# First attention of a fused attention and feed-forward kernel: a pair's sums behind the next pair's scores, loads ahead of them, a norm behind the last sums, and a load moved into the product

## The chip, the cores and the metric

The kernel runs on one core of one Trainium2 chip. The metric is the device time of one execution in microseconds (us). Times are medians over several executions. One profiled execution gives a trace; its span (first to last instruction) is some 1.8 us shorter than its time. Engines: PE (TensorE), DVE (VectorE), ACT (ScalarE), POOL (GpSimd), and SP, the queue that issues most transfers.

## The reference, cut to what matters

```python
# q, k, v: (8, 12, 448, 64) float32; w_in (768, 2048), w_out (2048, 768)
q_n, k_n = rmsnorm(q, g_q), rmsnorm(k, g_k)
scores = q_n @ k_n.T / sqrt(64)
attn = softmax(scores)              # division by the sum over keys, + 1e-9
x = (attn @ v) brought to (8 * 448, 768)
out = relu(x @ w_in) ** 2 @ w_out
```

## The kernel before

The work is done in spans of two batches. The two matrix products of a span are done with combined blocks, seven in place of eight; the combined weight blocks (`w1s`, `w2s`) are made once. So the first attention, 12 pairs of heads with nothing on PE but themselves, shares DVE, ACT and POOL with the making of the weights (`weights`, one quarter step, or tick, at a time). After it the first product starts, and PE is then full nearly all of the time (never idle from 220 to 1100 us).

The step of one pair, with the parts that the change touches:

```python
def norm(i):                                   # pairs 3 to 11 (first and later spans: other code)
    # ... ACT: squares
    nc.vector.tensor_reduce(rstd, ...)                                    # L694
    nc.vector.tensor_scalar(rstd, rstd, 1.0 / D, 1e-6, ALU.mult, ALU.add) # L695
    nc.gpsimd.tensor_tensor(flat, flat, mhalf[:SP, 0:4 * NJ], ALU.pow)    # L697
    nc.gpsimd.tensor_tensor(..q normalised.., ALU.mult)                   # L699

def add_up(i, c):                              # DVE: partial sums of the exponentials, L764
def total_of(i):                               # PE: sums over keys, by a matmul with ones, L815
def finish(i):                                 # DVE: 1/sum, spread, times the values, L828 to L835

def attention_alone():
    for i in range(NAT):                       # NAT = 12
        more = i + 1 < NAT
        scores(i, 0)
        scores(i, 1)
        # ... i == 0 apart
        if more:
            transpose(i + 1, 1, 0)             # k of the next pair
        if i + 3 < NAT:
            load(i + 3)
        values(i - 1, (2, 3))
        total_of(i - 1)
        add_up(i, 1)
        if i + 2 < NAT:
            norm(i + 2)
        elif not more:
            norm(NAT)                          # span 1's first pair
            load(NAT + 2)                      # span 1's third pair
        yield                                  # at each yield: one or two ticks of the weights
        if more:
            transpose(i + 1, 0, 0)             # q of the next pair: needs L699
        finish(i - 1)
        load_v(i + 1)
        yield
        scores(i, 2)
        scores(i, 3)
        values(i, (0, 1))
        yield
        if more:
            add_up(i, 2)
        combine_x(i - 1)
        # ...
        yield
    values(i, (2, 3))
    total_of(i)
    finish(i)
    combine_x(i)

# the first product, in turn with what is left of the weights
for u, _ in enumerate(first_product(work, 0)):
    # ...
    weights(min(ALL, EARLY + (ALL - EARLY) * (u - 1) // (N1 - 6)))   # EARLY = 4 * 12
```

Line numbers that the traces show: L749 scores, L737 transposes (copied by ACT, L739 and L741), L754 exponentials on ACT, L805 values, L815 sums, L764 adding up. The weights: L588, L593 and L598 on DVE, L563 and L569 on POOL. L646 loads a weight block (`sw`), L583 stores a finished group of blocks (`w1s`), L665 loads q and k of a pair of a later span.

## Time and profile before

| | kernel before |
|---|---|
| time, median (range) | 1401.76 us (1400.38 to 1402.51) |
| span of the profiled execution | 1402.8 us (its time: 1404.63) |
| PE busy | 98% |
| first matmul of the first product | 134.48 us |
| from there to the end | 1268.3 us |

From the table by stretches of time, the part after the attention (columns: stretch, length, PE, weight loads, DVE, ACT, POOL, clock of PE, DMA share, GB/s):

```profile
160.00:180.00 20.00, 19.52 (x52) 9.52 (x51) 15.18 (x20) 9.83 (x15) 17.18 (x18) 1.00 1.02 375
180.00:200.00 20.00, 19.44 (x52) 9.61 (x51) 13.96 (x18) 13.69 (x22) 15.82 (x16) 1.00 1.04 401
```

### The profile page before, as it was taken

Reading aid. Unit: us, or ns where it says so; the run is one execution under the profiler, and the core shown is the slowest. Engines: PE = TensorE matmul, PEld = TensorE weight load, DVE = VectorE, ACT = ScalarE, POOL = GpSimd, SP = SyncE. Lnnn points to the kernel's source line nnn. Section 1 sums busy time; section 2 is a strip of 40 time slices with the busy share of each in tenths; the row PEclk is TensorE's granted clock in tenths of the full one; section 3 lists DMA queues with packets and bytes.
Section 4 is the critical chain, followed back from the end, with each engine's and each line's share of the span. In section 5 each row is a group of like instructions: output and inputs, shape, how many; then the busy total and the mean of one; then the engine's idle time right before and its main releaser. Section 6 shows DMA issues by size and latency. Waiting matters only on the chain.

```text
span 1402.8 us, 14398 instructions
## 1 busy us (share of the span) xinstructions
PE 1378.1 (98%) x4426; PEld 635.5 (45%) x4426; DVE 814.3 (58%) x1404; ACT 420.3 (30%) x621; POOL 590.7 (42%) x400
## 2 busy tenths in 40 slices
PE   8989999999999999999999999999999999999997
PEld 3333444444444454544444455444444445554553
DVE  6989677589876234476767523457777633332111
ACT  7875555433322011233232011232323201110000
POOL 6998888544452022544353122445445302221000
PEclk9999999999999999999999999999999999999999
DMA  8676998645655333345565332344565343323443
GB/s 239 190 196 168 352 374 316 183 104 119 137 113 120 98 88 87 104 103 122 117 136 122 95 96 85 103 105 105 120 128 107 94 102 86 90 86 103 107 110 70
DMA packets 430914, 188.78 MB, mean 135 GB/s; under 512 B 277484, under 2 KB 428780, under 8 KB 430828
## 3 DMA queue, kind: packets, MB, share of 16 engines
q1 hardware_dynamic: 421228, 179.05, 49.3%
q10 hardware_dynamic: 9472, 8.72, 2.3%
q8 instruction: 37, 0.61, 0.2%
q14 instruction: 49, 0.40, 0.1%
q0 software_dynamic: 128, 0.00, 0.0%
HBM read 154.54 MB, written 33.16 MB: 134 GB/s over the span
## 4 chain that ended last, share of the span: by engine, by line
PE 89%; POOL 3%; DVE 3%; issue 1%; DMA 1%; ACT 1%; POOLq 0%; ACTq 0%
PE ps L1044 37%; PE pc L997 10%; PE pd L997 10%; PE pa L997 10%; PE sc L749 9%; PE pav L805 9%; PE pb L997 5%; DMA sw<-w1s 1%; DVE gT L764 1%; POOL rstd L697 1%; POOL gC L569 1%; POOL qk L699 1%; POOL gC L563 1%; DVE gC L598 0%; PE tot L815 0%
## 5 line engine op out<-in xcount | busy, mean ns | idle before, releaser
L1044 PE MATMUL ps<-gT,sw 128*128 128x448 f32 x768 | 299.2, 542 | 0.8 <-POOL gT L974 0.8
L719 POOL TENSOR_TENSOR half<-half,mhalf 128x28 f32<-128x28 f32 x36 | 173.6, 4824 | 262.3 <-DVE half L718 228.8
L1044 PE MATMUL ps<-gC,sw 128*128 128x448 f32 x576 | 225.2, 542 | 0.0
L974 POOL TENSOR_TENSOR gT<-gT 128x448 f32<-128x448 f32 x96 | 93.5, 976 | 311.9 <-ACT gT L970 311.9
L1044 PEld LDWEIGHTS ps<-gT,sw 128*128 128x128 f32 x768 | 143.9, 190 | 151.0 <-issue 146.5
L756 ACT ACTIVATE pr<-sc 112x896 f32<-112x896 f32 x120 | 104.8, 914 | 293.9 <-PE sc L749 201.7
L749 PE MATMUL sc<-qkT 64*112 64x448 f32 x768 | 171.5, 565 | 1.9 <-ACT gT L754 1.1
L1044 PEld LDWEIGHTS ps<-gC,sw 128*128 128x128 f32 x576 | 108.0, 190 | 112.3 <-issue 111.1
L997 PE MATMUL pa<-xT,sw 128*128 128x448 f32 x384 | 154.9, 539 | 0.5 <-DMA sw<-w1s 0.5
L970 ACT ACTIVATE gT<-gT 128x448 f32<-128x448 f32 x96 | 55.3, 576 | 312.6 <-DVE gT L1012 312.6
L749 PEld LDWEIGHTS sc<-qkT 64*112 64x112 f32 x768 | 61.2, 173 | 99.6 <-issue 81.5
L997 PEld LDWEIGHTS pa<-xT,sw 128*128 128x128 f32 x384 | 72.8, 190 | 72.5 <-issue 71.9
L805 PE MATMUL pav<-pr,vt 112*64 112x448 f32 x480 | 100.2, 547 | 0.0
L721 POOL TENSOR_TENSOR qk<-qk,half 128x448 f32<-128x448 f32 x72 | 84.3, 1191 | 2.8
L997 PE MATMUL pb<-xC,sw 128*128 128x448 f32 x192 | 77.6, 540 | 2.0 <-issue 1.5
L1012 DVE TENSOR_TENSOR gT<-z,pd 128x448 f32<-128x448 f32 x32 | 19.9, 621 | 102.2 <-PE pd L997 102.2
L764 DVE TENSOR_TENSOR acc<-acc,pr 112x896 f32<-112x896 f32 x60 | 68.3, 1138 | 18.4 <-ACT pr L756 15.9
L997 PE MATMUL pd<-xC,sw 128*128 128x448 f32 x192 | 77.5, 540 | 1.4 <-DMA sw<-w1s 1.3
L997 PE MATMUL pd<-xT,sw 128*128 128x448 f32 x192 | 78.0, 542 | 0.0
L997 PE MATMUL pc<-xC,sw 128*128 128x448 f32 x192 | 77.4, 539 | 0.0
L997 PE MATMUL pc<-xT,sw 128*128 128x448 f32 x192 | 77.4, 539 | 0.0
L569 POOL TENSOR_TENSOR gC<-gC 128x384 f32<-128x384 f32 x64 | 72.1, 1146 | 2.5
(120 smaller groups left out, 1565.7 us busy)
## 6 DMA issues: line engine op xcount, KB each, us to landing
sw<-w1s SPq DMA_DIRECT2D x224, 192.0 KB, 2.4
sw<-w2s SPq DMA_DIRECT2D x168, 256.0 KB, 3.3
w1s<-gC SPq DMA_DIRECT2D x8, 1344.0 KB, 7.5
w2s<-gC SPq DMA_DIRECT2D x8, 1344.0 KB, 5.7
out_dram<-osb SPq DMA_DIRECT2D x184, 56.0 KB, 1.9
qk<-in_q_dram SPq DMA_DIRECT2D x144, 56.0 KB, 3.0
qk<-in_k_dram SPq DMA_DIRECT2D x144, 56.0 KB, 2.9
vt<-in_v_dram SPq DMA_DIRECT2D x72, 112.0 KB, 2.9
```

Source lines behind the costliest of these rows:

```text
L569: nc.gpsimd.tensor_tensor(*[blocks_of(n)[:, i] for i in (dst, x, y)], op)
L719: nc.gpsimd.tensor_tensor(half, half, mhalf, ALU.pow)
L721: nc.gpsimd.tensor_tensor(qkn[:, s], raw[:, s], half[:, s * NG:(s + 1) * NG].rearrange("p g -> p g ()").to_broadcast([P, NG, 32]), ALU.mult)
L749: nc.tensor.matmul(sc[:, h, 0:S], qkT[rows, at, 1, c * SP:(c + 1) * SP], qkT[rows, at, 0, :], start=True, stop=True)
L756: nc.scalar.activation(pr, sc[:, :, 0:S], AF.Exp)
L764: nc.vector.tensor_tensor(acc, probs[i, 0] if c == 1 else acc, probs[i, c], ALU.add)
L805: nc.tensor.matmul(pavs[i][h * D:(h + 1) * D, :], vs[i][:, h, c, :], probs[i, c][:, h, :], start=(c == 0), stop=(c == NJ - 1))
L970: nc.scalar.activation(g, src, AF.Relu)
L974: nc.gpsimd.tensor_tensor(g, g, g, ALU.mult)
L997: nc.tensor.matmul(ps, stream[n + i][:, c], rhs[:, c], start=first and c == 0, stop=c == HC - 1, skip_group_check=not first)
L1012: add(g, x, ps, ALU.add)
L1044: nc.tensor.matmul(ps, stream[n][:, c % 4], rhs_of[i][:, c], start=c == 0, stop=c == HF - 1)
```

## The change

The intent: the sums over keys wait for DVE's adding up, so they go behind the next two scores; the loads go ahead of the scores; the norm of span 1's first pair leaves DVE's busy end of the attention; and the load that stood beside it goes into the product.

```diff
         for i in range(NAT):
             more = i + 1 < NAT
+            if 0 < i < NAT - 3:
+                load(i + 3)
             scores(i, 0)
             scores(i, 1)
 ...
             if more:
                 transpose(i + 1, 1, 0)
-            if i + 3 < NAT:
-                load(i + 3)
             values(i - 1, (2, 3))
-            total_of(i - 1)
             add_up(i, 1)
             if i + 2 < NAT:
                 norm(i + 2)
-            elif not more:
-                norm(NAT)
-                load(NAT + 2)
             yield
             if more:
                 transpose(i + 1, 0, 0)
-            finish(i - 1)
             load_v(i + 1)
             yield
             scores(i, 2)
             scores(i, 3)
+            total_of(i - 1)
             values(i, (0, 1))
+            finish(i - 1)
             yield
 ...
         finish(i)
         combine_x(i)
+        norm(NAT)
 ...
+                if u == 12:
+                    load(NAT + 2)
                 weights(min(ALL, EARLY + (ALL - EARLY) * (u - 1) // (N1 - 6)))
```

## The prediction

> **What bounds the kernel now.** I first read the page: TensorE (PE) is busy nearly throughout, so only its idle time can be won.
>
> ```profile
> PE 1378.1 (98%) x4426; PEld 635.5 (45%) x4426; DVE 814.3 (58%) x1404; ACT 420.3 (30%) x621; POOL 590.7 (42%) x400
> ```
>
> The span is 1402.8 us, so PE idles 24.7 us. The table by stretches of time says where: PE is short of full by 3.70, 1.99, 0.60, 0.50, 2.64, 3.52, 1.46, 1.30 us in the eight stretches of 20 us up to 160, 15.7 us in all; from 200 to 1200 it is never idle. The change touches just that part: the first attention (12 pairs, 9 to 134.5 us) and the head of the first product. So at most about 12 us (0.9%) can be had, since the first 3.7 us are start-up that the change leaves alone.
>
> Next, the same table shows what is full there:
>
> ```profile
> 40.00:60.00 20.00, 19.40 (x102) 7.20 (x100) 19.66 (x23) 16.35 (x28) 19.69 (x13) 1.00 0.58 173
> 60.00:80.00 20.00, 19.50 (x104) 7.38 (x102) 19.73 (x25) 16.79 (x28) 19.69 (x13) 1.00 0.65 186
> 100.00:120.00 20.00, 16.48 (x82) 5.90 (x82) 19.13 (x27) 12.55 (x22) 19.68 (x12) 0.95 0.54 148
> ```
>
> After the stretch and its length come PE, weight loads, DVE (VectorE), ACT, POOL (GpSimd), then PE's clock and the DMA share. PE, DVE and POOL are all full at once up to 80; from 100 to 120 PE has slack and POOL has none. The waits of PE from 0 to 260 us say what it sees:
>
> ```profile
> PE tot L815 <- DVE gT L764: 4.4, 5, 1.5
> PE pt L737 <- POOL qk L699: 2.2, 2, 2.0
> PE pb L997 <- issue: 1.5, 1, 1.5
> PE pd L997 <- DMA sw<-w1s: 1.3, 1, 1.3
> ```
>
> The first line is what the change aims at: the row sums (tot) wait for VectorE's adding up. The timelines of POOL and of PE around 116 us show who really sets the pace:
>
> ```profile
> 105.07 2.84 POOL L563 TENSOR_TENSOR gC<-gC 128x384 int32<-128x384 int32 x2
> 107.99 2.76 POOL L569 TENSOR_TENSOR gC<-gC 128x384 f32<-128x384 f32 x2
> 110.71 3.06 POOL L697 TENSOR_TENSOR rstd<-rstd,mhalf 112x16 f32<-112x16 f32 x1
> 113.85 2.64 POOL L699 TENSOR_TENSOR qk<-qk,rstd 112x512 f32<-112x512 f32 x1
> ...
> 112.82 1.68 PE L815 MATMUL tot<-gT,ones 112*64 112x448 f32 x8
> 116.55 0.60 PE L737 MATMUL pt<-ident,qk 112*128 112x112 f32 x4 [2.05 <-POOL qk L699]
> ```
>
> POOL runs without a gap: from 25.7 us (its first combined norm) to 127 it is idle only 0.54 us at 35 and 1.12 us at 86.9. A pair costs it a power (2.9 to 3.8), a normalising product (1.0 to 2.8) and four to six weight operations (1.0 to 2.0 each), 9.4 to 13.6 us; a pair costs PE 9.26 us (tot 70.69 to tot 79.95, no wait between). So PE can't run ahead: pair n's last transpose needs POOL's product (L699), which ends at 60.35, 71.7, 81.7, 91.5, 105.1 and 116.5 us. **POOL bounds the attention's second half**; the waits for tot are partly time that PE would have lost to POOL anyway.
>
> **What the Trainium skill says.** "SBUF — State Buffer", section "Who interferes with whom": a DVE instruction with two SBUF inputs contends with a GpSimd instruction that reads SBUF, and the later one blocks fully. The trace agrees: adding up (L764) takes 1.03 to 1.09 us where POOL is out of the way and 1.9 us where it isn't. So full DVE and POOL stretch each other; the change leaves the amount of such work alone. "TensorE: Matmul & The Clock Gate", "What's actually happening": activity sets the clock, over free-running windows of about 3.4 us. Here the granted clock was 0.54 and 0.61 in 118:120 and 120:122, after the wait of 2.05 us: the next 16 matmuls took 5.0 us in place of 3.3. "Trainium Kernel Development and Optimization", "Key Constraints": DMAs of all queues run on the same 16 engines; here weight blocks queue behind the 1344 KB stores, below.
>
> **The change, part by part.** The instruction order of the two kernels (compiled side by side) has the same instructions on every engine; only places differ.
>
> *Loads first.* In the SP queue's order no load of the first attention moves: the line moves within one step, and nothing else is issued in that step before it. Its waits (POOL's product, the reduce) stay too. Worth 0.
>
> *Sums behind the next scores.* PE's order per pair was scores, transpose, values, tot, transpose, scores, values; it becomes scores, transpose, values, transpose, scores, tot, values. Tot gains 2.2 us of room (transpose 0.53, scores 1.69), more than its longest wait of 1.53, so the 4.4 us vanish as named. But the transpose, which needs POOL, comes 1.65 us earlier and no longer has tot to fill its wait. Counting from each L699 end above: pair 6's transpose starts at 60.35, the next is ready at 69.6 and waits to 71.7 (2.1 us); the one after at 81.7 hardly waits; at 102.35 PE is ready and waits to 105.1 (2.8); at 114.6 it waits to 116.5 (1.9). After 116.5 PE owes, before: transpose 0.55, scores 1.69, values 1.65, scores 1.69, values 1.65, tot 1.67, scores 1.69, values 3.3, tot 2.45, sum 16.3, plus 1.6 of slow clock, 134.5. After: the same plus one tot, so the product starts near 136.2. **+1.7 us**, if POOL keeps its pace.
>
> *VectorE's tail.* finish of pair 9 started at 115.5, a little after its tot. Now that tot comes after the scores behind 116.5: with the slow clock 116.55 + 0.55 + 2.3 + 2.7 = 122. VectorE then does finish 2.5 (to 124.6) and all it did from 118.1 to 138.4 less the norm (2.5) and one wait (0.57), 17.2 us: finish of pair 11 ends at about 141.5 (140.2 at full clock) in place of 138.36. pb needs it: its bank held that pair's values, read at 137.40 to 138.36, and the wait of 1.5 before pb (138.46) is that. **pb at about 141, +2.6 us** in place of the hoped-for saving.
>
> *Norm behind the last sums.* It takes 2.5 us of VectorE and ACT's 1.9 us wait off that tail, counted above. But POOL's power (5.45) and products (1.84) now start at about 145 instead of 130.7, and stand in POOL's order before the totals of the next weight block. So the store of that block (issued 152.44) goes out at about 159, and the SP queue takes it before a block of weights:
>
> ```profile
> 152.44 0.41 SPq L583 DMA_DIRECT2D w1s<-gC  x1
> 153.80 2.57 SPq L646 DMA_DIRECT2D sw<-w1s  x2
> ...
> 153.80 9.51 DMA sw<-w1s
> 163.31 0.14 issue
> 163.44 1.74 PE pa L997 x4
> ```
>
> (timeline of the SP queue, then the chain of waits: issued 153.80, landed 163.31.) With 1.5 MB ahead at the 400 GB/s of this stretch, 3.8 us and some 2.5 more to land, that block comes at about 166 after the change: +2 to +3 us on 163.44. As PE is by then only level or 0.2 behind, this wait replaces the earlier delay and doesn't add to it.
>
> *The load moved to use 12.* It frees the SP queue of 3.9 us at 137 to 141, so the wait of 1.30 at 149 goes; this too is swallowed by the wait at about 164. At its new place (about 168 to 172) the DMA share is 1.0 and the eight small DMAs push weight blocks back; PE has five blocks of 2.25 us in hand. 0 to +1.
>
> **Sum.** +2.6 at the block that lands late, +0.5 for the moved load, -0.5 for the 0.56 us wait at 189 that may fall away: about +2.5 from the trace. Later code is the same and PE full, so it carries over one to one: 1401.76 + 2.5 = about 1404.
>
> **Rivals.** (a) *The intended gain comes*: tot's 4.4, pb's 1.5 and the DMA waits' 1.8 vanish, nothing takes their place, and no clock dip (1.6): 1401.8 - 9 = 1393 at best. For it: each wait is there by name. Against it: POOL's gapless chain to 116.5. Half of it, if POOL gets quicker by altered overlaps with VectorE, gives 1397 to 1399. (b) *It nets out*: the late store is hidden by better DMA order, the tail delay is 1 us: 1401 to 1402. (c) *The delays add*: late tail, late block, a second clock dip of 1.6 after the new 2.8 us wait at 102, and blocks starved by the moved load: 1408.
>
> **Range and chances.** Since the whole part holds 12 us of removable idle and the delays found are 1 to 6 us, nothing gets to 2% (28 us). I choose 1404.0 with 1398.5 to 1408.5; the low end covers half of rival (a). Faster by over 2%: 0.01; within: 0.98; slower: 0.01.
>
> **What would show it.** Right: PE's waits for tot near 0, its waits for POOL's L699 up from 2.2 to 5 us or more; L699's ends unchanged within 1.5 us; the product's first matmul at 135 to 137; pb at 140 to 142; a wait for a weight block of 2 to 4 us at about 164. Wrong: L699 ending for the last pair well before 116 (POOL was not the pace-maker), pb before 138, or the store that went out at 152.44 still going before 155.

## More of the kernel before

L997 (L995 or so in other kernels) is the first product.

## The result, and the profile after

The changed kernel is correct and takes 1408.77 us in the median (1408.30 to 1408.91, 4 runs), the kernel before on the same chip 1401.46 us (4 runs). A ratio here is of one kernel's runs to the other's of the same rounds, so it isn't quite the ratio of the medians quoted: 1.0052, with a 95% interval of 1.0034 to 1.0069, or some 7.3 us slower. That is within 2%, as predicted, but 0.27 us above the range given, and 4.8 us above the time given.

The profiled execution spans 1406.9 us. PE's line of the page:

```profile
PE 1377.0 (98%) x4426; PEld 636.0 (45%) x4426; DVE 812.7 (58%) x1404; ACT 420.4 (30%) x621; POOL 591.6 (42%) x400
```

The work is the same; the idle time of PE went from 24.7 to 29.9 us (1406.9 less 1377.0). The table by stretches says where (columns as above):

```profile
40.00:60.00 20.00, 20.00 (x104) 7.51 (x102) 19.62 (x22) 17.14 (x30) 19.46 (x12) 1.00 0.62 184
60.00:80.00 20.00, 18.18 (x96) 7.19 (x96) 19.66 (x22) 15.53 (x26) 19.66 (x12) 1.00 0.55 167
100.00:120.00 20.00, 17.30 (x92) 6.91 (x92) 16.58 (x22) 13.82 (x24) 19.69 (x12) 1.00 0.62 170
160.00:180.00 20.00, 16.29 (x42) 7.82 (x42) 13.73 (x19) 9.85 (x15) 19.53 (x20) 1.00 1.06 324
```

Two places are new: 60 to 80, where PE fell from 19.50 to 18.18 with DVE and POOL still full, and 160 to 180, where it fell from 19.52 to 16.29. What PE waits for (line, what released it, us in total, times, longest):

```profile
PE pt L737 <- POOL qk L699: 7.7, 6, 2.7
PE pd L995 <- DMA sw<-w1s: 3.1, 2, 2.4
PE pt L737 <- ACT qkT L739: 1.9, 1, 1.9
PE pa L995 <- ACT gT L968: 1.4, 1, 1.4
```

The waits for the sums (4.4 us before) are gone, and the waits for POOL's product took their place: 7.7 us where there were 2.2. The 1.9 us stand at 21 us, where the sums of the first pair used to fill a wait for ACT's copy. POOL still runs without a gap up to the last pair's product (timeline of POOL, then of PE):

```profile
105.36 2.84 POOL L563 TENSOR_TENSOR gC<-gC 128x384 int32<-128x384 int32 x2
108.29 2.76 POOL L569 TENSOR_TENSOR gC<-gC 128x384 f32<-128x384 f32 x2
111.01 2.91 POOL L697 TENSOR_TENSOR rstd<-rstd,mhalf 112x16 f32<-112x16 f32 x1
113.99 2.00 POOL L699 TENSOR_TENSOR qk<-qk,rstd 112x512 f32<-112x512 f32 x1
...
116.05 0.60 PE L737 MATMUL pt<-ident,qk 112*128 112x112 f32 x4 [1.26 <-POOL qk L699]
```

The second loss is in the SP queue (its timeline, then two links of the chain that ends in PE's wait at 198.00 us; that store went out as soon as POOL's work was done, and then took 10.46 us to land):

```profile
157.12 0.37 SPq L583 DMA_DIRECT2D w1s<-gC  x1
...
166.85 4.33 SPq L665 DMA_DIRECT2D qk<-in_q_dram  x4
171.23 3.35 SPq L665 DMA_DIRECT2D qk<-in_k_dram  x4
...
175.21 1.32 SPq L646 DMA_DIRECT2D sw<-w1s  x3
...
177.12 10.46 DMA w1s<-gC
187.64 10.22 DMA sw<-w1s
```

The moved load holds the queue for 7.7 us, at 166.85 to 174.6, in front of weight blocks. It took 3.9 us at its old place. The product runs short at 180.17 (2.44 us), 188.09 (0.92) and 198.00 (0.62).

### The profile page after: what moved, and what is told of

The parts are those of the page before. It is cut to its first block, busy times and chain, and to the rows that moved or that the text cites. A ratio compares the mean times of both kernels' runs of the same rounds, so it can differ in the third digit from the quotient of the medians. Undisturbed runs are those within 1.5% of the kernel's fastest.

```text
span 1406.9 us, 14401 instructions
## 1 busy us (share of the span) xinstructions
PE 1377.0 (98%) x4426; PEld 636.0 (45%) x4426; DVE 812.7 (58%) x1404; ACT 420.4 (30%) x621; POOL 591.6 (42%) x400
## 4 chain that ended last, share of the span: by engine, by line
PE 89%; DVE 4%; DMA 3%; ACT 1%; POOL 1%; issue 1%; SPq 0%; ACTq 0%; DVEq 0%; POOLq 0%
PE ps L1042 37%; PE sc L749 10%; PE pd L995 10%; PE pa L995 9%; PE pc L995 9%; PE pav L805 9%; PE pb L995 5%; DVE gT L764 1%; DMA qk<-in_k_dram 1%; DMA w1s<-gC 1%; DMA sw<-w1s 1%; PE tot L815 1%; DVE gC L598 1%; DVE rstd L694 0%; POOL rstd L335 0%
## 5 line engine op out<-in xcount | busy, mean ns | idle before, releaser
L764 DVE TENSOR_TENSOR acc<-acc,pr 112x896 f32<-112x896 f32 x60 | 68.2, 1136 | 18.1 <-ACT pr L756 15.6
L569 POOL TENSOR_TENSOR gC<-gC 128x384 f32<-128x384 f32 x64 | 76.6, 1216 | 2.5
```

Of the source, the lines that this page charges most:

```text
L569: nc.gpsimd.tensor_tensor(*[blocks_of(n)[:, i] for i in (dst, x, y)], op)
L764: nc.vector.tensor_tensor(acc, probs[i, 0] if c == 1 else acc, probs[i, c], ALU.add)
```

## The experiments

Every experiment below was timed in five rounds (c8 and s_early_fin have a sixth run; the changed kernel has four) against the kernel before on the same chip. Differences in us are the ratio less one, times 1402; the 95% intervals are about 1.9 us to each side (2.5 for the changed kernel). The ratios of the experiments agree with the listed times to 0.0001 when the first run of each list, the profiled one, is left out. With it, differences move by 0.8 us at most (e1_sums to +4.2, s_tail to +2.6). The kernel before itself spread from 1399.5 to 1405.1 us over all these runs.

| kernel | median us | ratio (95%) | difference | product starts | from there to the end |
|---|---|---|---|---|---|
| before | 1401.5 to 1402.8 | | | 134.5 | 1268.3 |
| changed | 1408.77 | 1.0052 (1.0034 to 1.0069) | +7.3 | 135.1 | 1271.9 |
| e1_sums | 1405.46 | 1.0025 (1.0011 to 1.0038) | +3.5 | 138.1 | 1268.2 |
| e3_load12 | 1404.67 | 1.0018 (1.0004 to 1.0031) | +2.5 | 133.5 | 1270.5 |
| e2_norm_load12 | 1404.59 | 1.0018 (1.0004 to 1.0031) | +2.5 | 131.3 | 1271.5 |
| f_load44 | 1401.72 | 0.9998 (0.9984 to 1.0012) | -0.3 | 131.4 | 1267.9 |
| f_all44 | 1405.01 | 1.0025 (1.0011 to 1.0039) | +3.5 | 135.1 | 1268.0 |
| s_head | 1405.25 | 1.0023 (1.0009 to 1.0036) | +3.2 | 136.1 | 1267.3 |
| s_tail | 1405.08 | 1.0024 (1.0010 to 1.0038) | +3.4 | (131.8) | (1266.9) |
| s_from2 | 1404.85 | 1.0023 (1.0010 to 1.0037) | +3.2 | 135.3 | 1268.7 |
| s_fin | 1406.53 | 1.0029 (1.0015 to 1.0043) | +4.1 | 138.4 | 1266.3 |
| s_early_fin | 1407.65 | 1.0034 (1.0019 to 1.0049) | +4.8 | 139.7 | 1266.8 |
| g_fast | 1402.12 | 1.0002 (0.9988 to 1.0016) | +0.3 | 131.3 | 1269.5 |
| g_sums_fast | 1398.15 | 0.9973 (0.9960 to 0.9987) | -3.8 | 127.8 | 1267.4 |
| c8 | 1398.13 | 0.9976 (0.9963 to 0.9989) | -3.4 | 122.1 | 1274.3 |
| c8_sums | 1400.93 | 0.9996 (0.9983 to 1.0010) | -0.6 | 124.4 | 1273.9 |
| c10_sums | 1401.98 | 0.9999 (0.9985 to 1.0013) | -0.1 | 132.6 | 1268.6 |
| c8_load44 | 1394.55 | 0.9944 (0.9930 to 0.9958) | -7.9 | 122.9 | 1269.8 |
| c10_load44 | 1393.30 | 0.9937 (0.9923 to 0.9950) | -8.8 | 126.6 | 1264.9 |
| c10_sumsy44 | 1397.13 | 0.9957 (0.9944 to 0.9970) | -6.0 | 132.3 | 1265.5 |

The last two columns are of the one profiled execution of each. That of s_tail was the odd one of its kernel (1400.49 us, the other four 1404.71 to 1406.43), so its columns stand in brackets and nothing is drawn from them.

A theory and two rivals stood at first: L, the load at use 12 costs most; S, the deferred sums cost most; N, the late norm does.

### One part at a time

"Loads ahead of the scores" alone needed no run: built alone, it gives the same instructions with the same waits on every engine as the kernel before.

**e1_sums**: sums and finish deferred, nothing else.

```diff
             values(i - 1, (2, 3))
-            total_of(i - 1)
 ...
-            finish(i - 1)
             load_v(i + 1)
             yield
             scores(i, 2)
             scores(i, 3)
+            total_of(i - 1)
             values(i, (0, 1))
+            finish(i - 1)
```

> Only the sums and the finish are put behind the next scores. Theory L (the load moved to use 12 costs most of the 7 us): +1 to +2 us on the kernel before, since the last pair's transpose still comes at about 116 us and one set of sums is now owed after it. Rival S (the deferred sums are the cost): +5 us or more. Rival N (the late norm is the cost): within 1 us of before. Waits of TensorE for tot near 0 in all three, waits for POOL's L699 above 5 us.

**e3_load12**: only the load moved to use 12.

```diff
                 norm(NAT)
-                load(NAT + 2)
 ...
+                if u == 12:
+                    load(NAT + 2)
```

> Only the third load of span 1 is moved to use 12 of the first product; norm and sums stay. Theory L: +2 to +4 us, with TensorE waiting 3 us or more for weight blocks between 170 and 200 us. Rivals S and N: -1 to 0 us, since the queue is freed at 137 us and the wait of 1.3 us at 149 goes.

**e2_norm_load12**: the same, and the norm behind the last sums (`+ norm(NAT)` after the last `combine_x`).

> The whole change without the deferred sums: norm behind the last sums, load at use 12. Theory L: +3 to +5 us. Rival S: within 1.5 us of before. Rival N: +5 us or more, and the difference to the run with the load alone at use 12 is 3 us or more.

**f_load44**: as e3_load12, with `u == 44` in place of 12.

> As the run before, but the load is moved to use 44 (about 235 us), where the DMA share falls below 1. Theory L: -1 to -2 us on before, 4 us or more better than with use 12. Rivals S and N: as with use 12, within 1 us.

Measured: +3.5, +2.5, +2.5 and -0.3 us. Rival N fell: with and without the late norm the time is the same. Theory L got its 2 to 4 us for the load, with waits for weight blocks of 2.4 us in place of 3 or more; rival S got less than its 5. So the loss has two parts of about the same size, deferral and load. They add to 6.0 of the 7.3, within the intervals. The last two columns of the table part them: with the load at use 12 the time from the product's start to the end is 1270.5 to 1271.9, without it, in all kernels with correct results and as much of the weights made early, 1266.3 to 1268.7. The deferral lies all in the product's start. e3_load12's PE timeline shows the short blocks at the places where the changed kernel has them:

```profile
176.40 2.49 PE L996 MATMUL pd<-xT,sw 128*128 128x448 f32 x6 [1.45 <-DMA sw<-w1s]
183.97 2.52 PE L996 MATMUL pc<-xT,sw 128*128 128x448 f32 x6 [0.57 <-DMA sw<-w1s]
193.88 2.49 PE L996 MATMUL pd<-xT,sw 128*128 128x448 f32 x6 [0.42 <-DMA sw<-w1s]
```

f_load44 missed what was expected of it, a gain of 1 to 2 us. It removes the cost of use 12 and no more, so the load at its old place cost nothing that can be measured.

**f_all44**: the whole change with the load at use 44.

> The whole change, but with the load of the first pair but two of span 1 at use 44 of the first product in place of use 12. If the parts add: 7.3 us (the whole change) less 2.9 us (use 12 against use 44, as measured on the kernel before) leaves +3.5 to +5 us against before. If the load at use 12 and the late norm only cost something because PE was already late, or the waits overlap: +6 us or more.

Measured +3.5, as the sum of the parts said; its PE has no wait for a weight block from 135 to 290 us. The load's place is thus worth 3.8 us within the change (0.0052 less 0.0025, times 1402). And the deferral with the late norm and the loads ahead costs what it costs alone (e1_sums, +3.5).

### Does POOL decide what the deferral is worth?

Theory P: the transposes need POOL's product, POOL is the pace, and a sum moved behind them only leaves the wait bare. Rival V: DVE and PE set the pace. Rival H: the early wait for ACT's copy at 21 us makes the cost.

**g_fast**: POOL's power on 4 of 16 columns, 1.25 us in place of about 3. Its output is wrong, which doesn't matter for the time.

```diff
-        nc.gpsimd.tensor_tensor(flat, flat, mhalf[:SP, 0:4 * NJ], ALU.pow)
+        nc.gpsimd.tensor_tensor(flat[:, 0:NJ], flat[:, 0:NJ], mhalf[:SP, 0:NJ], ALU.pow)
```

> The kernel before, with POOL's power on 4 of 16 columns of the norm of pairs 3 to 11 (wrong results on purpose), which takes some 2 us a pair from POOL and changes no other order. Theory P (POOL's gapless chain bounds the second half of the first attention): faster than before by 2 to 6 us, POOL idle before its powers, PE's waits for L699 near 0. Rival V (POOL is not the bound; VectorE and PE are): within 1 us of before.

**g_sums_fast**: the same, and the sums deferred as in e1_sums. Its output is wrong, which doesn't matter for the time.

> The same shortened power, with the sums deferred (wrong results on purpose); to be compared with g_fast. Theory P (deferred sums cost 3.4 us because the transposes then stand bare before POOL's product): with POOL relieved the deferral costs nothing or gains, g_sums_fast minus g_fast between -4 and +0.5 us. Rival V (the deferral costs by itself: one sum owed after the last transpose and VectorE's tail later): +2 to +4 us again. Rival H (the early wait of 1.94 us for ACT's copy and the slow clock after it): about +2.

Measured: +0.3 and -3.8. So half of theory P fell: relieving POOL alone brings nothing. The other half stood: with POOL relieved, deferring the sums is worth 4.1 us, where it costs 3.5 us without. The waits of PE in g_fast (first line) and in g_sums_fast (the other two) tell why:

```profile
PE tot L815 <- DVE gT L764: 6.5, 8, 2.0
...
PE pt L737 <- ACT qkT L739: 2.5, 1, 2.5
PE tot L815 <- DVE gT L764: 1.4, 2, 0.9
```

In g_fast no wait for POOL is left and the waits for the sums have grown from 4.4 to 6.5 us; DVE is busy 78.8 of the 80 us from 38 to 118 (74.2 in the kernel before). Part of that is stretching: the adding up takes 1.89 us in the mean, 1.60 in the kernel before. The product starts at 131.25 us, where f_load44, as fast as the kernel before, starts it at 131.43. DVE stands right behind POOL, the two are level as pace-makers, and taking one away shows the other. The deferral takes away the waits for DVE, and can win only where POOL doesn't give them back.

### Where in the deferral is the cost?

**s_head** and **s_tail**: the deferral for steps 1 to 6, or 7 to 11, alone (the old places if `i >= 7`, or `i < 7`).

> Sums and finish deferred for pairs up to 6 only (steps 1 to 6), correct results. Theory P (cost lies where PE waits for POOL, steps 7 to 11): 0 to +1 us against before. Rival H (cost comes from the early wait at 21 us): +2.5 to +3.5 us.

> Sums and finish deferred for steps 7 to 11 only, correct results. Theory P: +2.5 to +3.5 us against before. Rival H: 0 to +1 us.

**s_from2**: the deferral in all steps but the first.

> Sums and finish deferred in steps 2 to 11, step 1 as before. If the bare wait of step 1 makes the cost: at most +1.5 us against before. If POOL's chain or the late finish makes it: +2.5 to +3.5 us, as with all steps.

Measured +3.2, +3.4 and +3.2: neither theory for the halves, and for s_from2 the second of its alternatives. Rival H fell with s_from2, whose wait for ACT's copy is 0.8 us and whose cost is the same. The parts don't add up: each half costs as much as the whole. So it isn't a sum of bare waits, which my prediction had made it.

**s_fin**: PE's order as before, only finish moved.

```diff
             if more:
                 transpose(i + 1, 0, 0)
-            finish(i - 1)
             load_v(i + 1)
             yield
             scores(i, 2)
             scores(i, 3)
             values(i, (0, 1))
+            finish(i - 1)
```

> Only finish moved behind the values; the sums stay in their old place. If the late finish on VectorE (and what it overlaps on POOL) makes the cost: +2 to +3.5 us. If PE's order makes it (transposes bare, one sum owed): within 1 us of before.

**s_early_fin**: PE's order as in e1_sums, DVE's, POOL's and SP's orders as before (compared instruction by instruction). ACT's order is not as before: in seven steps four exponentials go ahead of an operation of the weights, so this run changes PE's order and a little of ACT's.

```diff
-            total_of(i - 1)
 ...
             if more:
                 transpose(i + 1, 0, 0)
+            scores(i, 2)
+            scores(i, 3)
+            total_of(i - 1)
             finish(i - 1)
             load_v(i + 1)
             yield
-            scores(i, 2)
-            scores(i, 3)
             values(i, (0, 1))
```

> Sums deferred behind the next pair's scores on PE, with VectorE's order as before: the two scores, the sums and finish stand ahead of the weights' step. If the late finish on VectorE made the cost: within 1.5 us of before, or faster by up to 2. If PE's order made it (bare transposes, a sum owed at the end): +2.5 to +3.5 us, as e1_sums.

Measured: +4.1 and +4.8. Finish moved alone costs all that the deferral costs, without any change to PE's order. And PE's order (with ACT's) costs it too with DVE's order untouched, where the theory of the late finish expected nothing. Neither is thus the cause by itself. The two have one thing in common: finish comes later on a DVE that has no time to give. In s_fin it slipped behind a step of the weights (L593, in some steps also L598) in DVE's order. In s_early_fin it kept its place in the order, so DVE stood still for it, 9.9 us in all (waits of DVE):

```profile
DVE gT L828 <- PE tot L815: 9.9, 6, 5.2
```

In the kernel before this wait doesn't show, and in f_load44 it is 0.2 us; in e1_sums, where finish both slips and waits, it is 7.3 us, in the changed kernel 4.1. What the slip does shows in the timelines of DVE and POOL at the same pair, 66 to 82 us; first f_load44, with finish (L828 to L835) at its old place:

```profile
66.99 1.08 DVE L764 TENSOR_TENSOR gT<-gT 112x896 f32<-112x896 f32 x1
68.45 1.09 DVE L764 TENSOR_TENSOR gT<-gT 112x896 f32<-112x896 f32 x1
70.41 2.35 POOL L569 TENSOR_TENSOR gC<-gC 128x384 f32<-128x384 f32 x2
71.82 0.64 DVE L828 STREAM_TRANSPOSE gT<-tot 128x448 f32<-128x448 f32 x1
```

and then s_fin:

```profile
67.94 0.64 DVE L828 STREAM_TRANSPOSE gT<-tot 128x448 f32<-128x448 f32 x1
70.41 1.47 DVE L764 TENSOR_TENSOR gT<-gT 112x896 f32<-112x896 f32 x1
70.88 4.14 POOL L569 TENSOR_TENSOR gC<-gC 128x384 f32<-128x384 f32 x2
72.27 1.90 DVE L764 TENSOR_TENSOR gT<-gT 112x896 f32<-112x896 f32 x1
```

With finish early, the adding up (L764, two inputs in SBUF) ran beside POOL's power and into its product and took 1.08 and 1.09 us (the product then took 1.77 us, in s_fin 1.04), and POOL's weights ran mostly beside DVE's transposes and reduces: 2.35 us for two. With finish late, it is finish that runs beside the power, and the adding up falls on POOL's weights: 1.47 and 1.90 us, and 4.14 for the two. This is what the Trainium skill's page "SBUF — State Buffer", section "Who interferes with whom", says of a VectorE instruction with two SBUF inputs beside a GpSimd instruction that reads SBUF: the two contend. The lines of the weights and of the product agree; beside the power, which reads SBUF too, no stretching shows (1.08 us, as with POOL idle at 23.2 us in the kernel before, 1.09). Over the stretch from 38 to 118 us (busy time of each group over its count, worked out from the timelines):

| mean us of one | finish at its old place (before, e2, e3, f_load44) | finish behind the values (changed, e1, s_fin, s_from2, f_all44) |
|---|---|---|
| DVE L764, adding up | 1.42 to 1.60 | 1.61 to 1.66 |
| DVE L598, weights | 0.95 to 0.99 | 1.23 to 1.28 |
| POOL L569, weights | 1.26 to 1.38 | 1.57 to 1.64 |
| POOL L699, product | 1.78 to 1.95 | 1.58 to 1.72 |
| POOL, end of the 2nd L699 to end of the last | 73.6 to 76.2 | 76.9 to 78.7 |

POOL's chain has the same instructions in the same order, with at most 1.4 us of waits in it, and is 2.4 us longer in the second group (the mean of 77.3 less that of 74.9). The two groups don't overlap, but 76.2 and 76.9 are close.

How a late POOL reaches the product shows in the SP queue. The v of the last pair stands there behind the loads of span 1's first pair, these behind a store of weights, and the store waits for two of POOL's totals (L569), which follow the last L699. First f_load44 (POOL, two lines of the queue, PE), then the changed kernel:

```profile
113.40 1.96 POOL L569 TENSOR_TENSOR gC<-gC 128x384 f32<-128x384 f32 x2
115.39 0.38 SPq L583 DMA_DIRECT2D w1s<-gC  x1
122.08 0.42 SPq L678 DMA_DIRECT2D vt<-in_v_dram  x1
125.37 3.73 PE L805 MATMUL pav<-gT,vt 112*64 112x448 f32 x16 [1.40 <-DMA vt<-in_v_dram]
...
115.95 3.68 POOL L569 TENSOR_TENSOR gC<-gC 128x384 f32<-128x384 f32 x2
119.66 0.38 SPq L583 DMA_DIRECT2D w1s<-gC  x1
126.35 0.42 SPq L678 DMA_DIRECT2D vt<-in_v_dram  x1
129.56 3.23 PE L805 MATMUL pav<-gT,vt 112*64 112x448 f32 x16 [1.38 <-DMA vt<-in_v_dram]
```

From the store to this v it is 6.7 us in all nine traces of the table. The v goes out at 122.1 to 125.1 us in the first group and at 125.4 to 128.2 in the second, 3.3 us later in the mean: 1.5 from the last L699 and 1.7 from the two totals behind it, which take 3.7 us in place of 2.0. PE waits for it 1.4 to 3.4 us in all of the nine but the kernel before, and the product starts 8.7 to 10 us after its issue (11.9 in s_fin, where PE ran at half clock after a wait of 3.4 us and the 16 matmuls took 6.17 us). These 3.3 us are of the size of the 3.2 to 4.1 us measured. The sum that PE owes after the last transpose is done before that wait, so in these traces it adds nothing to it. Each chain is of one execution.

What stays open: that the collisions make POOL's chain longer, and that this v carries the delay to the product, is read from timelines; no run took the collisions away and left the work, and none moved that v ahead of the store. The v isn't the whole of it either: in c8_sums and c10_sumsy44 (below) it goes out at 106.31 and 113.29 us, PE doesn't wait for it, and the deferral costs 2.8 us there too. In s_early_fin PE doesn't wait for it either; it comes to those values at 132.79 us, after a wait of 4.6 us for L699 at 108.55. POOL's chain is 76.6 us there, between the two groups, and its L569 takes only 1.45 us. And why half of the steps cost as much as all isn't shown.

### A version that beats both

If DVE and POOL tie, both must lose work (this also frees the SP queue, see below). `EARLY` sets how many of the weights' ticks go into the first attention. c8 is the kernel before with `EARLY = 4 * 8`, c8_sums the same with the sums deferred, c10_sums that with `4 * 10`.

```diff
-    EARLY, ALL = 4 * 12, 4 * (2 * NFC + 3)
+    EARLY, ALL = 4 * 8, 4 * (2 * NFC + 3)
```

> The kernel before with a third of the weights' work (16 of 48 ticks) taken out of the first attention and left to the first product; correct results. Theory T (POOL and VectorE tie as the pace, so only relieving both, or relieving POOL and deferring the sums, gains): 2 to 6 us faster, as both engines lose work. Rival F (the product lives on the blocks made early; the work and stores given back there make it wait): within 1 us or slower, with waits for weight blocks between 150 and 260 us.

> The same with the sums deferred. Theory T: at least as fast as c8, and 3 to 8 us faster than before. If the deferral's cost had nothing to do with the engines beside PE: 3 us slower than c8.

> Sums deferred with a sixth of the weights' work taken out (8 of 48 ticks). Theory T: between e1_sums (+3.4) and c8_sums, so about 0 against before.

Measured: -3.4, -0.6, -0.1. Theory T (in the texts above) held for c8 and c10_sums and missed for c8_sums. In c8 the waits for sums are down to 0.2 us, so the deferral had nothing left to win, and cost 2.8 us. Rival F was half right: c8's product starts 12 us earlier than before, and then takes 6 us longer, with 5.2 us of waits for weight blocks. So the load that stands in front of those blocks went to use 44, with `EARLY` at 8 and at 10:

> A third of the weights' work taken out of the first attention (as c8), with the load of span 1's third pair moved to use 44. c8 waits 5.2 us for weight blocks between 135 and 225 us; its load stands 4 us in the queue at 125 us. If that load pushes the blocks back: 1 to 3 us faster than c8, 1395 to 1397. If the blocks are short because they are made late: as c8 within 0.7 us.

> A sixth of the weights' work taken out, load at use 44. If what counts is the attention's engines being full: between f_load44 (-0.3) and c8_load44, 1398 to 1400.

Measured: -7.9 and **-8.8 us: 1393.30 us**, the fastest of all, correct, and within 0.7 us over five runs. Where the queue was the limit, use 44 was worth 4.5 us (c8 to c8_load44); on the kernel before it was worth nothing. Both did better than expected. A rival isn't ruled out: with less of the weights' work in the attention, the v of the last pair goes out at 105.34 and 108.34 us in these two (125.14 in the kernel before), and PE doesn't wait for it. How much of the gain is the queue's and how much the engines' no run shows. c10_load44's waits of PE from 10 to 290 us, none of them for a block:

```profile
PE tot L815 <- DVE gT L764: 2.5, 4, 1.3
PE pb L996 <- issue: 1.5, 1, 1.5
PE tot L815 <- DVE gT L828: 1.2, 1, 1.2
```

**c10_sumsy44**: c10_load44 with the sums deferred as in s_early_fin.

> c10_load44 (1393.3) with the sums deferred and VectorE's order kept. c10_load44's trace still waits 2.5 us for the adding up before the sums. If the deferral is harmless without the late finish: 1391 to 1394. If PE's order costs by itself: 1396 or more.

Measured: 1397.13, slower than c10_load44 by 2.8 us by the ratios (3.8 by the medians). Even here the deferral only costs.

## Why the prediction was wrong

- **Bound.** "POOL bounds the attention's second half" was half of it. POOL relieved alone gives nothing (g_fast), because DVE is level with it. The reading that an adding up of 1.03 to 1.09 us had POOL "out of the way" was wrong as well: POOL was at its power or at the start of its product then, as its own gapless chain says.
- **Loads first, 0.** Right: the same instruction streams.
- **Sums, +1.7 us.** The exchange was right: waits for tot gone, waits for L699 from 2.2 to 7.7 us. The size was off: +3.5 (e1_sums). The step that failed carried its own condition, "if POOL keeps its pace". I said of the contention that "the change leaves the amount of such work alone", which is true of the work and not of what it runs beside. Two of the six named ends of L699 came later by more than the 1.5 us allowed (83.25 for 81.7, 94.64 for 91.5), and finish moved alone costs as much as the whole deferral. The path to the product was wrong too: I let it run over the work that PE owes after the last transpose, one tot more. In the traces it runs over POOL's totals, the store and the v behind it, 3.3 us later with finish behind the values.
- **VectorE's tail, pb at about 141.** Wrong: 139.01, since PE kept its clock after the last wait of 1.26 us (the 1.6 us of slow clock after 116 us in the trace before did not come back): finish of pair 9 started at 120.04 in place of 122, and from there to the end of the last finish it took 18.9 us in place of 19.7 (2.5 and 17.2, which give 141.8 and not the 141.5 written).
- **Norm behind the last sums, +2 to +3.** The store did go late (157.12, predicted about 159), but the wait at 163.96 was 1.36 us and for ACT, and by e2_norm_load12 against e3_load12 the part costs nothing measurable in the end.
- **Load at use 12, 0 to +1.** This is the term that failed most: +2.5 us alone (e3_load12), 3.8 us against use 44 within the change. The place was predicted (168 to 172, measured 166.85 to 174.6), and so was the full DMA. The buffer of "five blocks of 2.25 us in hand" was taken as enough. It was not: the eight loads held the queue for 7.7 us, and the blocks behind them then waited for DMA engines already full. The wait of 1.30 us at 149 that the move takes away was worth nothing (f_load44: -0.3).
- **The sum.** I let the delays swallow each other, "replaces the earlier delay and doesn't add to it". Deferral and load add: they lie on either side of the product's start. Rival (c), 1408, was that, and its "blocks starved by the moved load" came.
- **The anchor.** The trace showed an execution that was 2.9 us slower than the median, clock dips and all. I took a difference against that trace and added it to the median. Trace against trace the change is +4.1 us, median against median +7.3.

## What to carry to other kernels

A wait that is there by name is worth only what the next engine in line doesn't take back: relieve one suspect alone and together with the change (here +0.3, and -3.8 in place of +3.5) before trusting it. On two engines that are full and get in each other's way, moving an instruction that has nothing to do with the collision can still cost, by what it pushes together (here +4.1 for finish alone; the way there is read from timelines). Where the next stage waits for a load, look at what stands before that load in its queue: here a store that waits for the busiest engine. Where a queue is in order and its stretch is full, move small loads to where the consumer is far ahead, and take work from the crowded part into the slack behind it: the two together, not the order within the crowd, gave the 8.8 us.

## What the Trainium skill lacked or had wrong

- "SBUF — State Buffer", section "Who interferes with whom": right in kind for POOL's weights and product. It names two factors of other measurements and no size for such a pair. Here an adding up took 1.09 us with POOL idle and 1.83 to 1.98 us in part or whole beside POOL's weights, and POOL's pair of weights operations 2.35 and 4.14 us. It makes no exception among GpSimd instructions that read SBUF, but beside a power (two inputs in SBUF) the adding up took 1.07 to 1.10 us, as with POOL idle.
- No page that I found gives the cost of a power on GpSimd: 112 x 16 elements took 2.9 to 3.8 us, 112 x 4 took 1.25 to 1.66 us.
- "Trainium Kernel Development and Optimization", section "Key Constraints": that DMAs share the 16 engines is stated and agrees; what a full stretch does to issuing is not. The same eight loads held the issuing queue for 3.9 us at 137 us (kernel before) and for 7.7 us at 167 us (changed kernel), with the DMA share at 1.06; two like sets of the kernel before took 6.1 us each, at 119 and 129 us.
